# One pass fewer in the conversion of 64-bit weights, the state's step as one instruction, and a new table for the order

## The chip, the cores and the metric

One Trainium2 chip, one core. The metric is device time in microseconds of one execution, the median of several runs. The core has five engines that run side by side, each through its own queue in order: TensorE (PE, matmuls), VectorE (DVE), ScalarE (ACT), GpSimd (POOL) and SyncE (SP), which here issues most DMAs. Semaphores tie the queues together.

## The reference

Three layers follow each other, and only the last one's result is returned.

```
state = 0                                         # per batch and head: 48 x 48
for t in range(768):                              # 4 batches, 8 heads
    y[t] = r[t] @ (state + (u * k[t]) x v[t])     # x: outer product
    state = w[:, None] * state + k[t] x v[t]
x = y as 3072 tokens of 384
h = x @ w_in                                      # 384 -> 1024
s = h * softmax(h);  ln = (s - mean(s)) / sqrt(var(s) + 1e-6) * g_ln
x = ln @ w_out                                    # 1024 -> 384
e = argmax(x @ w_gate);  p = softmax(x @ w_gate)[e]        # 8 experts
out = p * (relu(x @ w1[e]) @ w2[e])
```

`w_in` and `w_out` reach the kernel as 64-bit floats; everything else is 32 bits wide.

## The kernel before

Tokens go in 24 tiles of 128 (six to a batch). **The first stage** turns a tile of `r`, `k`, `v` (`load_rkv`, issued by SyncE) into attention output: `kpow`, `ruk`, `asum`, `aval` make the factors, `rtrans` and `ktrans` transpose on TensorE, `rev` and `kev` copy the transposes out (`rT`, `kT`), `scores` multiplies, `causal` masks the result into `AT` (L400), `ahi` and `alo` split it into two 16-bit parts, `vhi` and `vlo` do the same with `v`, `attend` multiplies with the values and with the decayed state, and `yout` adds it all up (L427). `update` makes the tile's `k x v`, `advance` (L439) adds it to the state in two instructions, one for each half of the partitions, and `decay` multiplies the state by its weights into `sdec`. The update is a block of 128x384 of which only the diagonal blocks are wanted; `wdec` is zero outside of them.

**The second stage** takes a finished tile through `xtrans`, `xhi`, `xlo`, `mm1` (18 matmuls, L474), `hmax`, `hexp`, `hsolu`, `hvar`, `hseed`, `zscale`, `zlo`, `ztrans`, `mm2` (24 matmuls, L559), `choose` to `place`, and `send`, which scatters the rows by expert to HBM. `mm1` needs all of `w_in`, `mm2` all of `w_out`.

**The weights** come in seven chunks, three of `w_in` (128x1024) and four of `w_out` (128x768). `conv` plans a load and the steps of `to_f32` for each; `to_f32` builds 32-bit floats from the two halves of each 64-bit word (`lo`, `hi`, every second word of `raw`): an absolute value on ScalarE (L167), then on VectorE a product that zeroes words too small for 32 bits (L169), two steps that place exponent, mantissa and sign (L172, L174) and one that adds the low bits (L176). `raw` has two buffers, `tmp` one. Then `win_hi`, `win_lo` (L191) split `w_in`, and `wout_g` to `wout_lo` (last step L253) scale, fold and split `w_out`.

**The third stage** runs the eight experts (`emm1`, `rhi`, `rlo`, `emm2`, `eout`, `esend`), with weights loaded and split by `weights`.

**A guard** stands beside this: `marks`, `flags` (TensorE, L658) and `judge` (VectorE, L664 to L675) make one flag from sums of squares, from `wbad` and from the counts of tokens. At the end every engine loads the flag (`values_load`, L1181) and, when it is set, a general path recomputes everything with plain loops. It isn't set for these inputs.

**The order** is written by a planner, `plan`: each step has an engine, a cost in us, predecessors and a due time, and a list schedule takes the step that can start first, ties within `EPS` by due time. The table `X` holds the due times' offsets and a few knobs (`DB` biases steps that may run on VectorE or GpSimd, marked "either"). The kernel issues its instructions in that order, and every engine's queue keeps it.

Of the kernel before, what the change touches and what calls it, by code (L numbers as in the profile page):

```python
# [8 lines left out]
F32 = mybir.dt.float32  # L9
# [6 lines left out]
AF = mybir.ActivationFunctionType  # L16
ALU = mybir.AluOpType
# [17 lines left out]
SA, SV, SZ, SW = 2.0 ** 10, 2.0 ** 9, 2.0 ** 8, 2.0 ** 10  # L35
# [5 lines left out]
def body(ctx, tc, r, k, v, w, u, w_in, w_out, g_ln, w_gate, w1, w2, out):  # L41
# [18 lines left out]
    def sml(name, slot=None):  # L60
# [24 lines left out]

    X = dict(ET=-429.78, GG=-233.7, SO=-294.91, FL=-505.75, OL=1, ybuf=10, tmp=1, rkv=3, LAT=0.06, SELF=0.05,
             PRE=1.4, EPS=0.06, TA=144.7, TB=237.7, TM=276.51, NA=8, NB=9, M0=1038.64, W0=81.15, TW=251.26,
             W1=-298.48, TV=171.34, PF=134.77, PW=224.32, F0=466.45, EL=3, e=3, S0=12.3, P0=10.1, D0=2.5,
             L0=140.96, L1=105.03, U0=108.15, KG=5.83, PT=2, ZT=-610.22, F2=261, TE=288.64, GA=-152.99,
             GW=-226.57, GN=-97.54, DB=-0.71, KS=5.09, K0=202.89, K1=-109.3, xtrans=-983.06, kev=-515.9,  # L90
             ahi=-247.51, vlo=-135.95, ruk=1202.87, attend=-89.6, choose=-323.29, xhi=-244.14, vhi=27.84,
             own=138.51, hvar=-317, hmax=-289.95, gexp=-194.8, ktrans=655.01, rtrans=830.4, hexp=357.44,
             ztrans=-337.98, asum=-344.06, rev=-225.55, xlo=-713.89, decay=439.69, alo=897.3, rank=107.2,
             ld=344.13, xrow=-508.46, mm2=767.79, causal=-1488.31, hseed=638.5, send=114.58, hsolu=83.6,
             yout=-62.13, zlo=360.17, scores=-213.79, square=539.99, place=100.24, ysquare=-70.93,
             advance=-563.07, update=-90.68, zscale=-828, hroot=-416.04, mm1=19.74, aval=-17.98, kpow=98.58)

# [23 lines left out]
    guard = const.tile([P, 2, NT], F32, name="guard")  # L121
    wbad = const.tile([P, 4], F32, name="wbad")
    ph1 = ctx.enter_context(ExitStack())
# [33 lines left out]

    def to_f32(t, n, is64, dst):

        dst.append(t[:, 0:n])  # L160
        if is64:
            words = t[:, 0:2 * n].bitcast(I32).rearrange("p (f w) -> p f w", w=2)
            lo, hi = words[:, :, 0], words[:, :, 1]
            tmp = cv.tile([P, 2, 1024], F32, tag="tmp", name="tmp", bufs=X["tmp"])
            hm, a = tmp[:, 0, 0:n].bitcast(I32), tmp[:, 1, 0:n].bitcast(I32)
            dst[-1] = a.bitcast(F32)
            A.activation(hm.bitcast(F32), hi.bitcast(F32), AF.Abs)  # L167
            yield
            V.scalar_tensor_tensor(hm.bitcast(F32), hm.bitcast(F32), 1.125 * 2.0 ** -15, hi.bitcast(F32),  # L169
                                   op0=ALU.is_ge, op1=ALU.mult)  # L170
            yield
            V.tensor_scalar(a, hm, 3, 0x3FFFFFF8, op0=ALU.logical_shift_left, op1=ALU.bitwise_and)  # L172
            yield
            V.scalar_tensor_tensor(a, hm, -0x40000000, a, op0=ALU.bitwise_and, op1=ALU.bitwise_or)  # L174
            yield
            V.scalar_tensor_tensor(a, lo, 29, a, op0=ALU.logical_shift_right, op1=ALU.bitwise_or)  # L176

    raw = {}
# [3 lines left out]

    def win_bits(c):
        raw["f", c] = f = []
        return to_f32(raw.pop(("i", c)), FF, w_in.dtype != F32, f)

# [8 lines left out]

    def wout_bits(c):
        raw["g", c] = f = []
        return to_f32(raw.pop(("o", c)), 2 * DM, w_out.dtype != F32, f)

# [79 lines left out]
    def tables():

        t4 = [P, 4]
        for j in range(2):
            SP.dma_start(out=wc[64 * j:64 * j + D, :], in_=w.rearrange("(j two) d -> two d j", two=2)[j])
        V.tensor_copy(wbad, wc)
        V.tensor_scalar(wc, wc, WLO, WHI, op0=ALU.max, op1=ALU.min)
        V.tensor_tensor(wbad, wbad, wc, op=ALU.not_equal)
        tt = rot.tile([P, 4, P], F32, name="tt", tag="kT")
# [624 lines left out]
    for i in range(NT):  # L912
# [422 lines left out]
```

## Time and profile before

| | us |
|---|---|
| median of 3 runs | 634.06 |
| lowest and highest run | 633.23, 634.15 |
| profiled execution | 634.09 |
| its span, first to last instruction | 632.4 |
| TensorE busy | 578.8 |
| VectorE busy | 455.9 |
| ScalarE busy | 347.9 |
| GpSimd busy | 272.0 |

The profiled execution lies 1.7 us above its span and agrees with the median. Busy shares over the whole span average three stages with different limits, so the profile is to be read stage by stage; the row of an engine's own wait names who ended it.

### The profile page before, as it was taken

To read this page: it belongs to the slowest core of one execution; us is meant where nothing else is said; L and a number is where in the kernel's file an instruction comes from. 1 tells how busy PE (TensorE), PEld (TensorE's weight loads), DVE (VectorE), ACT (ScalarE), POOL (GpSimd) and SP (SyncE) were. 2 spreads that over 40 slices of the span, in tenths; PEclk is the share of its full clock that TensorE was granted. 3 is DMA by queue.
4 is the path that set the end of the run, shared out by engine and by line. 5 is a ranking of instruction groups with operands and counts; after the bars stand their busy time and mean duration, and the time that the engine had idled before them with its cause. 6 is when DMAs were issued, how large, how long until landed. Compare 5 with 4: busy or idle time off the path is not lost.

```text
span 632.4 us, 10941 instructions
## 1 busy us (share of the span) xinstructions
PE 578.8 (92%) x4037; PEld 497.1 (79%) x4037; DVE 455.9 (72%) x799; ACT 347.9 (55%) x577; POOL 272.0 (43%) x435
## 2 busy tenths in 40 slices
PE   2767887999999999999999989999999999999992
PEld 2667776867777777778877648998889999999992
DVE  7999989998798888888875655447665767578010
ACT  2754557379777676777756753445252535345210
POOL 3778767746755865665535452110001021001211
PEclk9876978999999999999999989999999999999997
DMA  9943736994565592947044624735455675764110
GB/s 170 227 109 60 157 93 198 238 160 93 99 116 95 106 129 54 154 72 129 28 76 98 196 100 163 273 107 189 129 182 161 200 203 170 208 141 108 52 38 23
DMA packets 163185, 83.79 MB, mean 132 GB/s; under 512 B 140100, under 2 KB 156346, under 8 KB 162736
## 3 DMA queue, kind: packets, MB, share of 16 engines
q1 hardware_dynamic: 159808, 73.51, 51.7%
q0 software_dynamic: 3312, 9.47, 4.5%
q8 instruction: 34, 0.56, 0.4%
q14 instruction: 31, 0.25, 0.1%
HBM read 51.71 MB, written 16.30 MB: 108 GB/s over the span
## 4 chain that ended last, share of the span: by engine, by line
PE 52%; DVE 17%; issue 10%; DMA 10%; POOL 4%; ACT 4%; POOLq 0%; SPq 0%; ACTq 0%; DVEq 0%
PE emm L772 12%; PE mm L559 10%; PE mm L474 9%; DMA out<-o,gt 8%; PE emm L815 7%; PE emm L797 3%; PE scores L396 2%; PE update L433 2%; DVE AT L400 2%; PE attend L419 2%; DVE tmp L169 2%; DVE tmp L174 2%; PE etrans L753 1%; DVE vl L369 1%; PE attend L422 1%
## 5 line engine op out<-in xcount | busy, mean ns | idle before, releaser
L847 POOL DMA_INDIRECT out<-o,gt x30 | 30.1, 1003 | 206.8 <-ACT o L843 104.3
L559 PE MATMUL mm<-wo,zT 128*128 128x392 f16 x576 | 100.7, 332 | 0.5 <-DVE zT L550 0.4
L474 PE MATMUL mm<-wi,xh 128*128 128x512 f32 x288 | 91.8, 400 | 3.3 <-DVE AT L400 3.3
L559 PEld LDWEIGHTS <-zT 128*128 128x128 f16 x576 | 55.9, 98 | 38.4 <-issue 1.3
L783 ACT ACTIVATE hh<-emm 128x896 fp32r<-128x896 f32 (+7 forms) x32 | 28.2, 882 | 82.3 <-PE emm L772 79.6
L786 DVE SCALAR_TENSOR_TENSOR hl<-emm,hh 128x896 fp32r<-128x896 f32 (+7 forms) x32 | 33.4, 1044 | 55.2 <-ACT hh L783 55.2
L772 PE MATMUL emm<-exh,w1h 128*128 128x256 f32 (+8 forms) x216 | 73.1, 338 | 0.0
L772 PE MATMUL emm<-exh,w1l 128*128 128x256 f32 (+8 forms) x216 | 72.6, 336 | 0.0
L772 PE MATMUL emm<-exl,w1h 128*128 128x256 f32 (+8 forms) x216 | 72.6, 336 | 0.0
L474 PEld LDWEIGHTS mm<-wi,xh 128*128 128x128 f32 x288 | 52.7, 189 | 13.6 <-DVE AT L400 3.7
L474 PE MATMUL mm<-wi,xl 128*128 128x512 f32 x144 | 56.5, 392 | 0.0
L815 PE MATMUL emm<-hh,w2h 128*128 128x480 f32 (+4 forms) x120 | 43.8, 365 | 0.0
L815 PE MATMUL emm<-hh,w2l 128*128 128x480 f32 (+4 forms) x120 | 43.1, 359 | 0.0
L815 PE MATMUL emm<-hl,w2h 128*128 128x480 f32 (+4 forms) x120 | 43.1, 359 | 0.0
L613 POOL DMA_INDIRECT xs<-row,pos x24 | 29.7, 1236 | 30.0 <-issue 13.8
L396 PE MATMUL scores<-rT,kT 64*128 64x128 f32 x384 | 32.5, 317 | 11.0 <-DVE st L494 7.7
L772 PEld LDWEIGHTS emm<-exh,w1l 128*128 128x128 f32 x216 | 40.7, 189 | 1.4
L772 PEld LDWEIGHTS emm<-exh,w1h 128*128 128x128 f32 x216 | 40.8, 189 | 1.4
L772 PEld LDWEIGHTS emm<-exl,w1h 128*128 128x128 f32 x216 | 40.8, 189 | 1.3
L396 PEld LDWEIGHTS scores<-rT,kT 64*128 64x128 f32 x384 | 27.4, 216 | 15.4 <-issue 7.0
L500 ACT ACTIVATE z<-e,st 128x1024 f16<-128x1024 f32 x24 | 27.5, 1145 | 18.0 <-DVE st L494 11.0
L480 DVE TENSOR_REDUCE st<-mm 128x1 f32<-128x1024 f32 x24 | 29.3, 1220 | 10.6 <-PE mm L474 9.2
(208 smaller groups left out, 1566.0 us busy)
## 6 DMA issues: line engine op xcount, KB each, us to landing
stage<-in_moe_w SPq DMA_DIRECT2D x16, 768.0 KB, 4.8
stage<-in_moe_w SPq DMA_DIRECT2D x8, 1024.0 KB, 5.0
xs<-zf SPq DMA_DIRECT2D x8, 772.0 KB, 12.2
rkv<-in_r SPq DMA_DIRECT2D x24, 192.0 KB, 4.9
rkv<-in_k SPq DMA_DIRECT2D x24, 192.0 KB, 5.1
rkv<-in_v SPq DMA_DIRECT2D x24, 192.0 KB, 4.5
stage<-in_moe_w SPq DMA_DIRECT2D x8, 512.0 KB, 4.2
xg<-xs SPq DMA_DIRECT2D x5, 772.0 KB, 6.4
```

Of the source, the lines that this page charges most:

```text
L396: T.matmul(ps[:, a, j * P:(j + 1) * P], kT[h, j, :], rT[h, j, :], start=True, stop=True)
L474: T.matmul(ps[:, n, :], a[:, j, :], wi[b][:, j, n * 512:(n + 1) * 512], start=(j == 0 and m == 0), stop=(j == KD - 1 and m == 2))
L480: V.tensor_reduce(st[:, 0:1], tk["h", i], op=ALU.max, axis=AX.X, negate=True)
L500: A.activation(z[:, 0, :], tk["e", i], AF.Square, scale=-float(FF), bias=st[:, 2:3], accum_out=st[:, 4:5])
L559: T.matmul(ps[:, 0:OW], zz[:, a, c, :], wo[b][:, c, :], start=(c == 0 and m == 0), stop=(c == KF - 1 and m == 2))
L613: G.indirect_dma_start(out=xs, out_offset=bass.IndirectOffsetOnAxis(ap=pos.bitcast(U32), axis=0), in_=row, in_offset=None, bounds_check=E ...
L772: T.matmul(ps[:, x, :], a[:, j, fc * P:(fc + 1) * P], b[:, j, :], start=(j == 0 and m == 0), stop=(j == KD - 1 and m == 2))
L783: A.activation(cols(d, "hh", q), d["pm", q], AF.Relu)
L786: V.scalar_tensor_tensor(cols(d, "hl", q), d.pop(("pm", q)), 0.0, cols(d, "hh", q).bitcast(F32), op0=ALU.max, op1=ALU.subtract)
L797: T.matmul(ps[0:n, 0:DM], a[:, c, j * P:j * P + n], b[:, c, :], start=(c == 0 and m == 0), stop=(c == KF - 1 and m == 2))
L815: T.matmul(ps[:, 0:d["nr"]], a[:, c, m * P:(m + 1) * P], b[:, c, :], start=(c == 0 and x == 0), stop=(c == KF - 1 and x == 2))
L847: G.indirect_dma_start(out=out, out_offset=bass.IndirectOffsetOnAxis(ap=d["gt"][0:n, j, 1:2].bitcast(U32), axis=0), in_=d.pop(("o", j))[0: ...
```

## The change

`to_f32` drops the product L169. Two of the remaining three VectorE passes read `hi` in `raw` itself instead of the product in `tmp`. ScalarE, after the absolute value, computes Relu(threshold - |hi|) and sums it along the row into a new column of `wbad`, which grows from 4 to 12 columns; a sum above zero sets the guard's flag. On the general path (`small is None`) the four passes stay. `advance` becomes one instruction over all 128 partitions and 384 columns. The costs that the planner is told follow, `marks` waits for the conversions, and all of the table `X` is new.

```diff
-    wbad = const.tile([P, 4], F32, name="wbad")
+    wbad = const.tile([P, 12], F32, name="wbad")
+    thr = const.tile([P, 1], F32, name="thr")
...
+    G.memset(wbad, 0.0)
+    G.memset(thr, 1.125 * 2.0 ** -15)
...
-            V.scalar_tensor_tensor(hm.bitcast(F32), hm.bitcast(F32), 1.125 * 2.0 ** -15, hi.bitcast(F32),
-                                   op0=ALU.is_ge, op1=ALU.mult)
+            if small is None:
+                V.scalar_tensor_tensor(hm.bitcast(F32), hm.bitcast(F32), 1.125 * 2.0 ** -15, hi.bitcast(F32),
+                                       op0=ALU.is_ge, op1=ALU.mult)
+                hi = hm
+            else:
+                A.activation(hm.bitcast(F32), hm.bitcast(F32), AF.Relu, scale=-1.0, bias=thr, accum_out=small)
             yield
-            V.tensor_scalar(a, hm, 3, 0x3FFFFFF8, op0=ALU.logical_shift_left, op1=ALU.bitwise_and)
+            V.tensor_scalar(a, hi, 3, 0x3FFFFFF8, op0=ALU.logical_shift_left, op1=ALU.bitwise_and)
             yield
-            V.scalar_tensor_tensor(a, hm, -0x40000000, a, op0=ALU.bitwise_and, op1=ALU.bitwise_or)
+            V.scalar_tensor_tensor(a, hi, -0x40000000, a, op0=ALU.bitwise_and, op1=ALU.bitwise_or)
             yield
             V.scalar_tensor_tensor(a, lo, 29, a, op0=ALU.logical_shift_right, op1=ALU.bitwise_or)
...
     def advance(i):
-        p4 = tk.pop(("pu", i))[:, 0:DM].rearrange("p (j a d) -> p j a d", j=4, a=2)
-        for a in range(2):
-            h = slice(64 * a, 64 * a + 64)
-            if i % NC == 0:
-                V.tensor_scalar(state[h, :, a, :], p4[h, :, a, :], SV, None, op0=ALU.mult)
-            else:
-                V.scalar_tensor_tensor(state[h, :, a, :], p4[h, :, a, :], SV, sdec[h, :, a, :], op0=ALU.mult, op1=ALU.add)
+
+        flat, ps = state.rearrange("p j a d -> p (j a d)"), tk.pop(("pu", i))[:, 0:DM]
+        if i % NC == 0:
+            V.tensor_scalar(flat, ps, SV, None, op0=ALU.mult)
+        else:
+            V.scalar_tensor_tensor(flat, ps, SV, sdec.rearrange("p j a d -> p (j a d)"), op0=ALU.mult, op1=ALU.add)
...
-        op(("bits", kind, c), "", [("act", 1.15 * t), ("dve", 1.4 * t), ("dve", 1.3 * t), ("dve", 1.4 * t), ("dve", 1.4 * t)] if F64 else [("dve", .01)],
+        op(("bits", kind, c), "", [("act", 1.15 * t), ("act", 1.15 * t), ("dve", 1.1 * t), ("dve", 1.4 * t), ("dve", 1.4 * t)] if F64 else [("dve", .01)],
...
-            op(("advance", i), "dve", .71, [("update", i), ("decay", i - 1), ("decay", i - 2)], advance, i, first=f + X["advance"])
+            op(("advance", i), "dve", .55, [("update", i), ("decay", i - 1), ("decay", i - 2)], advance, i, first=f + X["advance"])
...
-    X = dict(ET=-429.78, GG=-233.7, SO=-294.91, FL=-505.75, OL=1, ybuf=10, tmp=1, rkv=3, LAT=0.06, SELF=0.05,
+    X = dict(ET=-29.23, GG=-120.46, SO=-383.87, FL=374.6, OL=1, ybuf=10, tmp=1, rkv=3, LAT=0.06, SELF=0.05,
...
```

Where instructions stand now, at three places.

VectorE at the beginning, from the last of the tables (`trT`, L313) into the first tiles, before:

```order
L313 TENSOR_SCALAR trT<-trT 128x512
L627 MEMSET koff 128x1
L169 SCALAR_TENSOR_TENSOR tmp<-tmp,raw 128x1024
L172 TENSOR_SCALAR tmp<-tmp 128x1024
L347 TENSOR_TENSOR kp_116<-rkv_118,tkm 128x8x48
L369 SCALAR_TENSOR_TENSOR vl<-rkv_118,vh 128x384
L383 TENSOR_TENSOR rT<-rtrans,trT 128x512
L174 SCALAR_TENSOR_TENSOR tmp<-tmp 128x1024
L442 TENSOR_SCALAR state<-update 64x4x48 x2
```

and after, where `trT` (L322) is thirteen instructions ahead of the first L181 and the rows begin with the first tile's `au`:

```order
L366 TENSOR_REDUCE au<-ru 128x8
L378 SCALAR_TENSOR_TENSOR vl<-rkv_122,vh 128x384
L409 TENSOR_TENSOR AT<-scores,mask 128x1024
L392 TENSOR_TENSOR rT<-rtrans,trT 128x512
L366 TENSOR_REDUCE au<-ru 128x8
L418 TENSOR_TENSOR al<-AT,ah 128x1024
L409 TENSOR_TENSOR AT<-scores,mask 128x1024
L181 TENSOR_SCALAR tmp<-raw 128x1024
L392 TENSOR_TENSOR rT<-rtrans,trT 128x512
L183 SCALAR_TENSOR_TENSOR tmp<-raw,tmp 128x1024
L452 SCALAR_TENSOR_TENSOR state<-update,sdec 128x384
L185 SCALAR_TENSOR_TENSOR tmp<-raw,tmp 128x1024
```

The first pass over a chunk stood directly behind the tables (a memset apart) and stands behind the first attention steps of two tiles now; the three passes follow each other within five rows.

VectorE at the end of the program, where `hl` is a step of the last expert and `fli` the guard's flag, before:

```order
L786 SCALAR_TENSOR_TENSOR hl<-emm_6679,hh 128x2x368
L786 SCALAR_TENSOR_TENSOR hl<-emm_6703,hh 128x2x368
L786 SCALAR_TENSOR_TENSOR hl<-emm_6726,hh 128x2x368
L786 SCALAR_TENSOR_TENSOR hl<-emm_6750,hh 128x2x368
L1181 TENSOR_LOAD fli
```

and after, where the last `hl` and the first of `judge` (L672) stand just ahead:

```order
L673 TENSOR_SCALAR guard<-flags 128x24
L674 TENSOR_REDUCE fl<-guard 128x1
L675 TENSOR_SCALAR fl<-fl 128x1
L676 TENSOR_TENSOR guard<-keys,kcap 128x8
L677 TENSOR_SCALAR guard<-flags 128x1
L678 TENSOR_REDUCE fl<-guard 128x1
L679 TENSOR_SCALAR fl<-flags 128x1
L680 TENSOR_TENSOR fl<-fl,flags 128x1
L681 TENSOR_TENSOR fl<-fl 128x1
L682 TENSOR_TENSOR fl<-fl 128x1
L683 CAST fli<-fl 128x1
L1189 TENSOR_LOAD fli
```

The instructions of `judge` stood within the first expert before and are VectorE's last now, ahead of its load of the flag.

TensorE at the end of the program, where `emm` is the last expert's second product, before:

```order
L797 MATMUL emm_6831<-w2h,hl 112x384
L797 MATMUL emm_6831<-w2h,hh 112x384
L797 MATMUL emm_6831<-w2l,hh 112x384
L797 MATMUL emm_6831<-w2h,hl 112x384
L1181 TENSOR_LOAD fli
```

and after:

```order
L805 MATMUL emm_6798<-w2l,hh 112x384
L805 MATMUL emm_6798<-w2h,hl 112x384
L666 MATMUL flags<-guard,mask 128x48
L667 LDWEIGHTS ones_71
L667 MATMUL flags<-cum,ones_71 128x8
L668 LDWEIGHTS ones_71
L668 MATMUL flags<-cuma,ones_71 128x1
L1189 TENSOR_LOAD fli
```

The matmuls of `flags` moved from the first expert's first product to behind the last expert's last matmul.

## Rows read from the trace of the kernel before

**Rows 1.** The page's part 2: busy tenths of VectorE in 40 equal slices.

```profile
DVE  7999989998798888888875655447665767578010
```

**Rows 2.** Busy time by stage (stretch, length, engines, granted clock, DMA share, GB/s).

```profile
9.20:134.50 125.30, 100.14 (x842) 89.09 (x843) 120.14 (x163) 70.61 (x121) 87.68 (x73) 0.88 0.75 159
...
134.50:378.00 243.50, 237.14 (x1836) 179.27 (x1837) 193.87 (x410) 177.98 (x315) 146.11 (x306) 0.99 0.56 104
...
378.00:620.60 242.60, 241.50 (x1361) 228.73 (x1358) 136.16 (x188) 96.60 (x140) 34.53 (x41) 1.00 0.51 152
```

**Rows 3.** VectorE's groups, 0 to 134.5 us (busy us, mean ns | idle before).

```profile
L400 DVE TENSOR_TENSOR AT<-scores,mask 128x1024 f32<-128x1024 f32 x10 | 12.2, 1218 | 0.4 <-PE scores L396 0.3
...
L369 DVE SCALAR_TENSOR_TENSOR vl<-rkv,vh 128x384 f16<-128x384 f32 x11 | 12.1, 1096 | 0.3 <-ACT vh L365 0.3
...
L169 DVE SCALAR_TENSOR_TENSOR tmp<-tmp,raw 128x768 f32<-128x768 f32 (+1 forms) x7 | 11.1, 1581 | 0.1
...
L383 DVE TENSOR_TENSOR rT<-rtrans,trT 128x512 f32<-128x512 f32 x10 | 6.8, 680 | 0.4 <-PE rtrans L374 0.4
...
L357 DVE TENSOR_REDUCE au<-ru 128x8 f32<-128x384 f32 x11 | 6.0, 543 | 0.1
...
L444 DVE SCALAR_TENSOR_TENSOR state<-update,sdec 64x192 f32<-64x192 f32 x16 | 5.6, 350 | 0.9 <-PE update L433 0.8
...
L427 DVE SCALAR_TENSOR_TENSOR av<-attend,av 128x384 f32<-128x384 f32 x10 | 5.5, 550 | 1.0 <-PE attend L422 0.8
...
L361 DVE TENSOR_TENSOR av<-rkv,au 128x384 f32<-128x384 f32 x6 | 5.1, 862 | 0.0
```

**Rows 4.** Lines of the conversion (ns: least, median, most; first, last start).

```profile
L169 DVE SCALAR_TENSOR_TENSOR tmp<-tmp,raw x7: 949/1256/3149, 9.8 to 107.1; 128x768 f32<-128x768 f32 x4, 128x1024 f32<-128x1024 f32 x3
...
L172 DVE TENSOR_SCALAR tmp<-tmp x7: 545/1022/2321, 11.0 to 108.4; 128x768 int32<-128x768 int32 x4, 128x1024 int32<-128x1024 int32 x3
...
L176 DVE SCALAR_TENSOR_TENSOR tmp<-raw,tmp x7: 943/1208/1732, 20.7 to 113.3; 128x768 int32<-128x768 int32 x4, 128x1024 int32<-128x1024 int32 x3
```

**Rows 5.** Timeline of VectorE and TensorE (start, length); last, a piece of the chain.

```profile
9.77 1.22 DVE L169 SCALAR_TENSOR_TENSOR tmp<-tmp,raw 128x1024 f32<-128x1024 f32 x1
...
10.95 1.09 PE L374 MATMUL rtrans<-ident,rkv 128*128 128x128 f32 x4 [0.62 <-ACT tkm L312]
...
134.52 8.12 PE L559 MATMUL mm<-wo,zT 128*128 128x392 f16 x48
...
166.30 0.36 PE L419 MATMUL attend<-sdec,rT 128*128 128x96 f32 x2
...
168.00 0.52 PE L457 MATMUL xtrans<-ident,av 128*128 128x128 f32 x3
...
172.78 0.60 PE L379 MATMUL ktrans<-ident,kp 128*128 128x128 f32 x4
...
173.13 0.71 PE L474 MATMUL mm<-wi,xh 128*128 128x512 f32 x2
...
177.41 1.16 PE L396 MATMUL scores<-rT,kT 64*128 64x128 f32 x16
...
194.26 0.86 PE update L433 x8
```

**Rows 6.** The flag and the end (timeline; last two: ns, then start us).

```profile
385.73 0.32 PE L658 MATMUL flags<-guard,mask 128*128 128x48 f32 x2
...
387.97 0.15 DVE L675 CAST fli<-fl 128x1 int32<-128x1 f32 x1
...
620.27 0.34 PE L797 MATMUL emm<-w2h,hl 128*112 128x384 f32 x1
...
622.17 0.95 POOL L847 DMA_INDIRECT out<-o,gt  x1 [2.75 <-DMA out<-o,gt]
...
L1181 POOLq TENSOR_LOAD <-fli x1: 504/504/504, 622.0 to 622.0; - x1
...
L1183 POOLq EVENT_SEMAPHORE  x6: 17/30/43, 625.3 to 625.7; - x6
```

More of the change, by code (lines that the diff above doesn't have):

```diff
@@ L84, in body @@
     V.memset(mhalf, -0.5)
-    X = dict(ET=-429.78, GG=-233.7, SO=-294.91, FL=-505.75, OL=1, ybuf=10, tmp=1, rkv=3, LAT=0.06, SELF=0.05,
[L87 to L96, printed above, removed]
@@ new lines, in body @@
+    X = dict(ET=-29.23, GG=-120.46, SO=-383.87, FL=374.6, OL=1, ybuf=10, tmp=1, rkv=3, LAT=0.06, SELF=0.05,
+             PRE=1.4, EPS=0.1, TA=176.56, TB=248.64, TM=254.17, NA=8, NB=9, M0=495.42, W0=42.93, TW=105,
+             W1=-530.44, TV=257.99, PF=664.51, PW=-382.4, F0=-386.07, EL=3, e=3, S0=12.3, P0=10.1, D0=2.5,
+             L0=-679.5, L1=615.58, U0=13.12, KG=9.92, PT=2, ZT=-247.56, F2=148.59, TE=84.91, GA=118.81,
+             GW=-220.86, GN=157.31, DB=-1.5, KS=8.04, K0=610.2, K1=199.94, xtrans=-970.71, kev=571.15,
+             ahi=622.76, vlo=9.17, ruk=307.19, attend=625.35, choose=-170.33, xhi=-20.99, vhi=706.01,
+             own=263.22, hvar=668.67, hmax=132.27, gexp=-753.32, ktrans=-390.29, rtrans=539.68, hexp=150.63,
+             ztrans=70.39, asum=173.22, rev=-2168.6, xlo=-650.67, decay=77.28, alo=655.25, rank=-472.96,
+             ld=-228.91, xrow=-249.65, mm2=1203.62, causal=-107.84, hseed=-596.66, send=-284.2, hsolu=-201.28,
+             yout=597.49, zlo=288.89, scores=540.82, square=141.08, place=-51.35, ysquare=-575.28,
+             advance=-342.55, update=136.08, zscale=-399.78, hroot=-622.85, mm1=452.87, aval=631.76,
+             kpow=460.49)
@@ L156, in raw_load, with to_f32 @@
         return t
-    def to_f32(t, n, is64, dst):
+    def to_f32(t, n, is64, dst, small):
         dst.append(t[:, 0:n])
@@ L181, in win_load, with win_bits @@
         raw["i", c] = raw_load(w_in, c, 1)
-    def win_bits(c):
+    def win_bits(c, count=True):
         raw["f", c] = f = []
-        return to_f32(raw.pop(("i", c)), FF, w_in.dtype != F32, f)
+        return to_f32(raw.pop(("i", c)), FF, w_in.dtype != F32, f, wbad[:, 4 + c:5 + c] if count else None)
     def win_hi(c):
@@ L194, in wout_load, with wout_bits @@
         raw["o", c] = raw_load(w_out, c, 2)
-    def wout_bits(c):
+    def wout_bits(c, count=True):
         raw["g", c] = f = []
-        return to_f32(raw.pop(("o", c)), 2 * DM, w_out.dtype != F32, f)
+        return to_f32(raw.pop(("o", c)), 2 * DM, w_out.dtype != F32, f, wbad[:, 8 + c // 2:9 + c // 2] if count else None)
     def wout_g(c):
@@ L259, in fold_all @@
             win_load(c)
-            run(win_bits, c)
+            run(win_bits, c, False)
             win_hi(c)
@@ L264, in fold_all @@
             wout_load(c)
-            run(wout_bits, c)
+            run(wout_bits, c, False)
             wout_g(c)
@@ L283, in tables @@
             SP.dma_start(out=wc[64 * j:64 * j + D, :], in_=w.rearrange("(j two) d -> two d j", two=2)[j])
[L284 removed]
+        V.tensor_copy(wbad[:, 0:4], wc)
         V.tensor_scalar(wc, wc, WLO, WHI, op0=ALU.max, op1=ALU.min)
[L286 removed]
+        V.tensor_tensor(wbad[:, 0:4], wbad[:, 0:4], wc, op=ALU.not_equal)
         tt = rot.tile([P, 4, P], F32, name="tt", tag="kT")
@@ L970, in body @@
     b_left = set(ops)
-    last = [(n, i) for n in ("place", "ysquare", "square", "causal") for i in range(NT)]
+    last = [("bits", "i", c) for c in range(KD)] + [("bits", "o", c) for c in range(0, KF, 2)] + [(n, i) for n in ("place", "ysquare", "square", "causal") for i in range(NT)]
     op("count", "pe", .06, [("place", i) for i in range(NT)], count, bank="s", until=[("sort", 0)], first=X["SO"])
```

## The prediction

> **What bounds the kernel now.** I read the busy shares along the span first, then the same by stage. VectorE is at nine tenths or more in nearly all of the first eight slices of forty [rows 1]. Cut where TensorE starts its first `mm2` (134.52 us [rows 5]), the stages have different limits [rows 2]: from 9.2 to 134.5 us VectorE is busy 120.1 of 125.3 us while TensorE has 100.1, at a granted clock of 0.88; from 134.5 to 378 us TensorE is busy 237.1 of 243.5 us, VectorE 193.9; from 378 to 620.6 us TensorE has 241.5 of 242.6. So the end is the first `mm2` plus a nearly full TensorE, and a VectorE instruction is worth its length only before 134.5 us. The profiled execution took 634.09 us for a span of 632.4, the median of the runs is 634.06: a change of the span is a change of the time.
>
> **The removed pass.** The seven L169 instructions cost 11.1 us in that stage [rows 3]. They range from 949 to 3149 ns [rows 4]. Undisturbed they would be four of 0.95 and three of 1024 columns at 1.22 (the AT pass of that size [rows 3]), 7.5 us; the other 3.6 us are waits. Because a GpSimd instruction that held L169 up may hold up the next VectorE instruction instead, I give half back: 1.8 us, bounds 0 and 3.6.
>
> What the trace shows is a spread of one shape by more than three. The Trainium skill, "SBUF — State Buffer", section "SBUF: two separate sides", says that VectorE and GpSimd lock a port pair for a whole instruction, and that a VectorE instruction with two SBUF inputs is of the kind that must wait. The rows agree as far as they go: L444, with one input from PSUM, shows none of the spread in its mean of 350 ns. By that page two of the three passes that stay have two SBUF inputs as well; if all 3.6 us came back through them, the time would be 630.9 us.
>
> **The first remaining pass** now reads every second word (`hi` in `raw`) where L172 read a packed tile. At the plain rate a stride costs nothing visible: L176 reads `lo` that way and has 943 ns at the least. But L172's least is 545 ns, a faster form [rows 4]. Kept, the cost is 0; lost, four times 0.40 and three times about 0.2 (1.22 against the median of 1.02), 2.2 us. I take 0, because nothing else in the instruction changes, and keep 2.2 as the other end.
>
> **ScalarE** gets seven Relu with a sum, about as long as the seven Abs of L167 plus 0.19 for reading the accumulator: 8 us. It is busy 70.6 of 125.3 us in the stage [rows 2], and nothing but the next use of `tmp` waits for them: cost 0; without that cover it would be up to 8 us, one per chunk.
>
> **The state's step.** Two halves of 0.35 us become one of 128x384, for which yout (L427, one PSUM and one SBUF input, same size) has 0.55 [rows 3]: 0.15 us saved each. Twenty steps, of which only those before the first `mm2` count.
>
> **The order** is the larger part. Counted along VectorE's rows up to the last `wo` low part (L253, L262 after), the new order has done less attention by then. Before and after: AT 10 and 8, `vl` 11 and 8, `rT` 10 and 8, `au` 11 and 8, yout 9 and 5, `av` on VectorE 6 and 1, steps of the state 9 and 6, `al` on VectorE 0 and 2. By [rows 3]: L169 -11.1; the state 18 halves at 0.35 against 6 at 0.55, -3.0; `vl` -3.3; AT -2.4; `rT` -1.4; `au` -1.6; yout -2.2; `av` -4.3; `al` +2.4 (two at the 1.22 of an AT pass). Six other kinds change by one or two short instructions, three up and three down, and are left out as cancelling. Sum -26.9 us.
>
> Against that stands the start. Before, VectorE fills its wait for the first tile with conversion. After, the conversion begins thirteen instructions behind the tables, and the first of these needs the first transposed tile, whose transposes run from 10.95 to 12.04 us [rows 5], while L169 starts at 9.77 [rows 5]: 2.2 us idle, and I add 0.8 where the first AT waits for scores. So +3.0, bounds 0 and 4.
>
> First `mm2`: 134.5 - 26.9 + 1.8 + 3.0 = 112.4 us. TensorE then owes what was put off. Its own order at the first `mm2`, before and after: `mm1` 6 and 5, scores 10 and 8, update 10 and 7, `rtrans` and `ktrans` 11 and 8 each, `xtrans` 8 and 5, attend 10 and 8. Start to next start in a gapless stretch [rows 5]: `mm1` 4.28, attend 1.70, four transposes 0.35; scores 1.16, `xtrans` 0.52, update 0.86 as listed. 4.28 + 2 x 1.16 + 3 x 0.86 + 6 x 0.35 + 3 x 0.52 + 2 x 1.70 = 16.2 us. The state of 134.5 us is reached at 112.4 + 16.2 = 128.6: **5.9 us gained**. Nothing of it is the mere shift of work.
>
> The steps of the second stage stay on a TensorE with 6.4 us idle [rows 2], so the saving there is 0; the expert stage has 1.1 us idle, so its other interleaving is 0.
>
> **The end.** `flags` and `judge` leave 385.7 us for the place behind the last matmul of TensorE. Before, every engine loaded the flag when it ran out of work, GpSimd last: load at 622.0 us for 0.50, and its next event behind the branch at 625.3 [rows 6]. Now no engine can branch before `judge` is done. From the first flags matmul (385.73) to the end of the last judge row (387.97 + 0.15) are 2.39 us; the last expert matmul starts at 620.27, so flags at about 620.44, judge done 622.83, load over at 623.33 against 622.46: **+0.9 us**. Bounds: 0, if the last send (issued at 622.17) sets the end, and 2.4, if all of judge comes on top.
>
> What the trace shows is 2.8 us from GpSimd's branch at 622.5 to its next event. The Trainium skill, "Runtime: NRT & Kernel Launch", section "Instruction fetch mechanics", says that a taken branch out of the prefetched window must fetch its target first. This speaks against the change: all five engines would fetch at once. The row agrees with a fetch, no row shows five together; with the 2.4 of the bound the time would be 630.6 us.
>
> **Sum.** 634.09 - 5.9 + 0.9 = **629.1 us**. With the poor ends (1.8 more wait, 2.2 for the stride, 1.0 at the start, tail 2.4) it is 634.09 - 0.9 + 2.4 = 635.6; with the good ones (1.8, 3.0, tail 0) 634.09 - 10.7 = 623.4.
>
> **Rivals.**
> A, forecast: 625.5 to 632.8 us, chance 0.46.
> B, the good ends together: 623.4, below 625.5, chance 0.17. For it: 25 us of TensorE idle and the clock of 0.88 before the first `mm2` [rows 2]; a denser feed would also give clock back. Against: VectorE's new start.
> C, the pass is gone but its time isn't: GpSimd's holds move on, the stride loses the fast form, the tail eats the rest (0.9 gained, 0.9 lost): 634.1, within 0.2%, chance 0.17. That is also the case in which the three passes cost what four did.
> D, slower: TensorE starves in the second stage because attention runs less far ahead. Counted in its order, before the seventh `mm1` 10 tiles are attended before and 8 after; before the tenth 12 and 11; before the thirteenth 15 and 13. A late tile costs its `mm1` yout 0.55, transposes 0.52 and a ScalarE copy and a VectorE subtraction of the same 384 columns, about 0.55 each (estimate from yout): 2.2 us at most. Half of the 18 that follow paying 1.3 gives 11.7 us: 634.1 - 5.0 + 11.7 = 640.8. It decides from 6.3 us of new waits, 0.35 for each. For it: VectorE also inherits the put-off attention there and is 80% busy now; against: the idle of only 6.4 us shows that such waits are rare. Chance 0.20.
>
> **How the numbers follow.** Likeliest is A at 629.1. 0.2% is 1.3 us, about what a measurement of this kernel can tell from no change. Faster: A and B, 0.63; same: C, 0.17; slower: D, 0.20. The range 622.5 to 638.5 leaves out some 0.06 of B and 0.11 of D.
>
> **What would show it.** Right: the first `mm2` at 110 to 116 us; no fourth pass and VectorE still over 90% busy before; ScalarE up 8 us and no row waiting for its Relu; the second stage's TensorE idle at 5 to 9 us; judge as the last VectorE rows and 10 to 11 us after them. Wrong: a first `mm2` after 120 us (the start or the waits are larger), the first pass of 768 columns at 0.95 instead of 0.55, TensorE idle over 12 us in the second stage (D), or over 14 us from the last expert matmul to the end.

## The result, and the profile after

| | us |
|---|---|
| before, median of 6 runs (lowest, highest) | 634.11 (633.23, 634.94) |
| after, median of 6 runs (lowest, highest) | 628.51 (628.42, 631.10) |
| ratio, 95% interval | 0.9916, 0.9904 to 0.9928 |
| profiled execution of after, its span | 629.15, 627.4 |

The change makes the kernel 5.6 us faster; 629.1 was forecast. Executions of one kernel spread by 2 to 7 us here, the long ones mostly with a lower granted clock (last section), so each median below is given with its lowest and highest. Here are the busy times by stage after the change, cut at the first `mm2`, at the second stage's last row copy (`xrow`) and at the last expert copy (`o`). The columns are those of [rows 2].

```profile
9.20:116.30 107.10, 80.62 (x671) 70.00 (x671) 98.07 (x131) 68.93 (x112) 70.76 (x63) 0.87 0.70 170
116.30:373.60 257.30, 254.55 (x2023) 195.28 (x2024) 210.79 (x433) 189.42 (x337) 146.73 (x312) 1.00 0.51 107
373.60:613.20 239.60, 238.51 (x1345) 226.96 (x1343) 132.94 (x173) 96.54 (x141) 35.05 (x36) 1.00 0.52 153
```

The kernel before has the first of these cuts in [rows 2]; the other two there:

```profile
134.50:380.50 246.00, 239.64 (x1852) 180.84 (x1853) 195.01 (x413) 177.98 (x315) 148.45 (x311) 0.99 0.55 104
380.50:620.70 240.20, 239.02 (x1346) 227.17 (x1343) 135.02 (x186) 96.60 (x141) 32.20 (x37) 1.00 0.51 153
```

Stage by stage: 18.2 us less to the first `mm2`, 11.3 more from there to the last `xrow`, 0.6 less among the experts. From the last `o` to the end of the span it was 632.4 - 620.7 = 11.7 us and is 627.4 - 613.2 = 14.2, so 2.5 more. Sum: -18.2 + 11.3 - 0.6 + 2.5 = -5.0, the difference of the two spans.

VectorE's groups of the first stage after the change (busy us, mean ns | idle before), to be read against [rows 3, 4]:

```profile
L409 DVE TENSOR_TENSOR AT<-scores,mask 128x1024 f32<-128x1024 f32 x8 | 9.7, 1216 | 0.2
...
L378 DVE SCALAR_TENSOR_TENSOR vl<-rkv,vh 128x384 f16<-128x384 f32 x8 | 6.6, 830 | 4.5 <-ACT vh L374 4.5
...
L185 DVE SCALAR_TENSOR_TENSOR tmp<-raw,tmp 128x1024 int32<-128x1024 int32 x3 | 6.5, 2162 | 0.0
...
L200 DVE TENSOR_TENSOR wi<-tmp,wi 128x1024 fp32r<-128x1024 f32 x3 | 6.3, 2109 | 0.5 <-ACT wi L197 0.5
...
L183 DVE SCALAR_TENSOR_TENSOR tmp<-raw,tmp 128x1024 int32<-128x1024 int32 x3 | 4.5, 1513 | 0.0
...
L181 DVE TENSOR_SCALAR tmp<-raw 128x768 int32<-128x768 int32 x4 | 2.8, 706 | 0.0
...
L452 DVE SCALAR_TENSOR_TENSOR state<-update,sdec 128x384 f32<-128x384 f32 x5 | 2.7, 543 | 0.0
```

L181, L183 and L185 are the three passes, L452 is the state's step. `vl` has an idle of 4.5 us in front of it that no row of before has. Where it stands is seen in VectorE's timeline at the start (start, length, idle before):

```profile
6.02 0.10 DVE L302 TENSOR_TENSOR tt<-tt 128x4 f32<-128x4 f32 x1
10.57 0.56 DVE L378 SCALAR_TENSOR_TENSOR vl<-rkv,vh 128x384 f16<-128x384 f32 x1 [4.45 <-ACT vh L374]
11.05 0.16 DVE L302 TENSOR_TENSOR tt<-tt 128x4 f32<-128x4 f32 x1
...
14.24 0.42 DVE L322 TENSOR_SCALAR trT<-trT 128x512 f32<-128x512 f32 x1
17.30 0.69 DVE L392 TENSOR_TENSOR rT<-rtrans,trT 128x512 f32<-128x512 f32 x1 [2.64 <-PE rtrans L383]
```

and in ScalarE's:

```profile
7.58 1.28 ACT L353 ACT_TABLE_LOAD   x1 [7.58 <-DMA rkv<-in_v]
8.87 1.16 ACT L353 ACTIVATE sq<-rkv 128x1152 bf16<-128x1152 f32 x1
...
10.04 0.51 ACT L374 ACTIVATE vh<-rkv 128x384 f16<-128x384 f32 x1
```

The first tile's `vl` stands in the middle of the tables (VectorE's powers of the decay, `tt` to `trT`). It waits for `vh`, which stands behind a load of ScalarE's own function table (1.28 us) and a square on ScalarE, and these wait for the load of `v`. The tables are done at 14.7 us instead of 9.85, and the first `rT` starts at 17.3 instead of 14.06.

The end, by each queue's branch behind the flag (line; count: ns; start) and the event that follows it:

```profile
L1191 SPq EVENT_SEMAPHORE  x9: 17/17/17, 620.2 to 620.8; - x9
L1191 POOLq EVENT_SEMAPHORE  x6: 17/30/43, 620.3 to 620.8; - x6
...
L1191 ACTq EVENT_SEMAPHORE  x2: 17/17/17, 619.7 to 619.8; - x2
L1191 DVEq EVENT_SEMAPHORE  x2: 21/21/21, 621.3 to 621.4; - x2
L1191 ACTq COMPARE_BRANCH  x1: 50/50/50, 616.1 to 616.1; - x1
L1191 POOLq COMPARE_BRANCH  x1: 53/53/53, 616.1 to 616.1; - x1
L1191 SPq COMPARE_BRANCH  x1: 53/53/53, 616.2 to 616.2; - x1
L1191 PEldq COMPARE_BRANCH  x1: 3369/3369/3369, 616.3 to 616.3; - x1
L1191 DVEq COMPARE_BRANCH  x1: 72/72/72, 616.5 to 616.5; - x1
```

All branch within 0.4 us of each other. GpSimd's next event comes 4.2 us behind its branch, where it was 2.8 [rows 6]. In between, the core's DMA engines carry instructions: six packets start between 617.05 and 617.56 us, within 1.5 us of the branches, and the longest lasts 2.1 us, up to 619.6. The earliest of the next events stands at 619.7. The view of 617 to 618 us (packets, MB, share of the engines):

```profile
q14 instruction: 5, 0.04, 24.6%
q8 instruction: 1, 0.02, 6.4%
```

### The profile page after: what moved, and what is told of

Read it like the earlier page. It is cut to its first block, busy times and chain, and to the rows that moved or that the text cites. A ratio compares the mean times of both kernels' runs of the same rounds, so it can differ in the third digit from the quotient of the medians.

```text
span 627.4 us, 10956 instructions
## 1 busy us (share of the span) xinstructions
PE 573.8 (91%) x4037; PEld 492.2 (78%) x4037; DVE 448.2 (71%) x781; ACT 357.1 (57%) x591; POOL 256.3 (41%) x428
## 5 line engine op out<-in xcount | busy, mean ns | idle before, releaser
L855 POOL DMA_INDIRECT out<-o,gt x30 | 33.0, 1100 | 202.4 <-ACT o L851 98.4
L482 PE MATMUL mm<-wi,xh 128*128 128x512 f32 x288 | 93.8, 408 | 0.6 <-DVE AT L409 0.6
L482 PEld LDWEIGHTS mm<-wi,xh 128*128 128x128 f32 x288 | 54.1, 194 | 11.4 <-DVE AT L409 0.8
L621 POOL DMA_INDIRECT xs<-row,pos x24 | 28.3, 1179 | 24.7 <-issue 13.8
L528 ACT ACTIVATE e<-e,st 128x1024 f32<-128x1024 f32 x22 | 27.3, 1241 | 19.4 <-POOL st L524 19.4
L428 PE MATMUL attend<-sdec,rT 128*128 128x96 f32 x160 | 36.7, 316 | 0.1
L717 DVE TENSOR_TENSOR w2l<-stage,w2h 128x768 fp32r<-128x768 f32 x32 | 30.1, 950 | 8.2 <-ACT w2h L715 8.2
L715 ACT ACTIVATE w2h<-stage 128x768 fp32r<-128x768 f32 x32 | 26.1, 842 | 14.0 <-PE emm L823 13.2
```

The source lines that it names most:

```text
L428: T.matmul(ps[:, j * 96:j * 96 + 96], rT[:, j, :], sdec[:, j].rearrange("p a d -> p (a d)"), start=True, stop=False, skip_group_check=True)
L482: T.matmul(ps[:, n, :], a[:, j, :], wi[b][:, j, n * 512:(n + 1) * 512], start=(j == 0 and m == 0), stop=(j == KD - 1 and m == 2))
L528: A.activation(e, e, AF.Identity, scale=st[:, 10:11], bias=st[:, 11:12])
L621: G.indirect_dma_start(out=xs, out_offset=bass.IndirectOffsetOnAxis(ap=pos.bitcast(U32), axis=0), in_=row, in_offset=None, bounds_check=E ...
L717: V.tensor_tensor(lo, d[:, x], hi.bitcast(F32), op=ALU.subtract)
L855: G.indirect_dma_start(out=out, out_offset=bass.IndirectOffsetOnAxis(ap=d["gt"][0:n, j, 1:2].bitcast(U32), axis=0), in_=d.pop(("o", j))[0: ...
```

## The experiments

The mark used below is the start of the first `mm2`, besides the time; in the changed kernel it is 116.34 us. A ratio is to the kernel before, measured beside it, with its 95% interval.

**1. The code in the old order.** The table and the planner's costs of before (and its predecessors of `marks`) under the changed code; one pass is moved by hand.

```
-    X = dict(ET=-29.23, GG=-120.46, SO=-383.87, FL=374.6, OL=1, ybuf=10, tmp=1, rkv=3, LAT=0.06, SELF=0.05,
+    X = dict(ET=-429.78, GG=-233.7, SO=-294.91, FL=-505.75, OL=1, ybuf=10, tmp=1, rkv=3, LAT=0.06, SELF=0.05,
...
     order, done = plan()
+    row = next(r for r in order if r[2] == (("bits", "i", 0), 2))
+    order.remove(row)
+    order.insert([r[2] for r in order].index(("rev", 0)) + 1, row)
```

> The changed code (three passes, the Relu count, the state's step as one instruction) in the order of before: its table and the costs its planner was told; only the first pass of the first chunk stands three rows later, behind the first rT, because it would otherwise stand ahead of the tables. Theory 1, what VectorE saves before the first mm2 reaches the end where the order doesn't give it away: L169 -11.1, half of its waits back +1.8, nine state steps -1.35, about +1.5 at the start where L169 and L172 filled a wait: first mm2 at about 125.3 us, and as TensorE's order is the same it owes nothing: 634.1 - 9.2 = 625 us. Theory 2, TensorE or the loads hold the stage as soon as VectorE is shorter: half of it, first mm2 at 129 to 130, 629 to 630 us. Theory 3, the gain of the changed kernel is the order's: 632 to 634 us.

Measured: 629.99 us (627.59 to 632.02), ratio 0.9938 (0.9919 to 0.9957), first `mm2` at 129.1. Theory 2. The first stage:

```profile
9.20:129.10 119.90, 95.01 (x842) 83.55 (x842) 108.93 (x140) 77.56 (x134) 85.59 (x73) 0.91 0.80 166
```

VectorE's busy time fell by 11.2 us, but its idle time rose from 5.2 to 11.0, so that only 5.4 us arrived at the first `mm2`. What it waited for:

```profile
DVE kp L355 <- ACT tkm L320: 5.3, 1, 5.3
DVE st L487 <- PE mm L481: 3.7, 2, 2.5
```

**2. The same with the start mended,** because `tkm` had come to stand behind the first Relu. The first chunk's Relu and two passes, the first square, `vh` and `vl` go behind the first `kT`.

```
     order, done = plan()
+    row = next(r for r in order if r[2] == (("bits", "i", 0), 1))
+    order.remove(row)
+    order.insert([r[2] for r in order].index(("kev", 0)) + 1, row)
...
```

> As code_only (the changed code in the order of before), with its start mended: the first chunk's Relu and the first tile's square and vh stand behind the first kT on ScalarE, so that tkm doesn't wait for them, and the first two passes and vl follow there on VectorE. In code_only VectorE waited 5.3 us for tkm and its first rT started at 16.5 us instead of 14.1. Theory 1: the 2.4 us come back, first mm2 at about 126.7, 627.5 us median; the new order is then worth nothing as it stands, and 5 us with its own start and tail mended (both). Theory 2, the old order loses them later in the stage (VectorE waited 3.7 us for mm1 in code_only): first mm2 at 129, 630 us. Theory 3, the old order is as good once the code is there: 623 us, the same as both.

Measured: 629.30 us (628.41 to 631.15), ratio 0.9929 (0.9907 to 0.9950); the first `rT` starts 4.2 us earlier than in experiment 1 (12.22 against 16.47 us), the first `mm2` at 129.4. Theory 2: the old order loses the start again, later in the stage.

```profile
9.20:129.40 120.20, 99.11 (x842) 87.21 (x843) 107.46 (x140) 77.33 (x134) 84.12 (x73) 0.89 0.81 166
```

VectorE is idle for 12.7 us. What it waited for:

```profile
DVE st L487 <- PE mm L481: 3.6, 2, 2.5
DVE vl L377 <- ACT vh L373: 2.4, 2, 2.2
DVE kp L355 <- DMA rkv<-in_k: 2.3, 1, 2.3
```

TensorE has the same 842 matmuls in front of the first `mm2` as before and needs 99 us of these 120 for them at a granted clock of 0.89. So in the old order no one engine holds this stage. That TensorE's longer list is what eats the saving is likely, but no run tests it by itself.

**3. The new order with the old code,** four passes and halves of the state.

```
-                A.activation(hm.bitcast(F32), hm.bitcast(F32), AF.Relu, scale=-1.0, bias=thr, accum_out=small)
+            V.scalar_tensor_tensor(hm.bitcast(F32), hm.bitcast(F32), 1.125 * 2.0 ** -15, hi.bitcast(F32),
+                                   op0=ALU.is_ge, op1=ALU.mult)
+            hi = hm
...
```

> The order of the changed kernel with the code of before (four passes with the product L169, no Relu, the state's step in two halves). Theory 1: seven products (11 us) and seven second halves (1 us) come back before the first mm2, which moves from 116.3 to about 128.5 us, and the end by as much: 640 us, so that the order alone would be a loss of 6. Theory 2, the first stage has slack and half of it is hidden: 634 us. Theory 3, the order alone is the gain: 630 us or less.

Measured: 639.86 us (639.51 to 641.42), ratio 1.0092 (1.0075 to 1.0109), first `mm2` at 126.8. Theory 1: the order alone loses 5.7 us, and in this order the code is worth 11.3 us (639.86 - 628.51). By the ratios, each to the kernel before on its own chip, it is 11.2 us, or 9.9 with the second set of the changed kernel (0.9936, experiment 6). In the old order it was worth 4.2 (experiment 1) and 5.4 (experiment 2).

```profile
9.20:126.80 117.60, 85.08 (x672) 72.40 (x673) 107.69 (x145) 61.48 (x98) 70.14 (x63) 0.85 0.65 155
```

The product's seven rows in this order:

```profile
L174 DVE SCALAR_TENSOR_TENSOR tmp<-tmp,raw 128x768 f32<-128x768 f32 x4 | 4.5, 1130 | 0.0
...
L174 DVE SCALAR_TENSOR_TENSOR tmp<-tmp,raw 128x1024 f32<-128x1024 f32 x3 | 4.3, 1424 | 0.0
```

Only 672 matmuls stand ahead of the first `mm2`, 85.1 of 117.6 us, and what the code saves on VectorE (107.7 - 98.1 = 9.6 us busy) arrives: with the new code the first `mm2` starts 10.5 us earlier.

**4. The start of the changed kernel mended:** the first `vl` behind the first `rT`, the second square behind the first `kT`.

```
     order, done = plan()
+    row = next(r for r in order if r[2] == ("vlo", 0))
+    order.remove(row)
+    order.insert([r[2] for r in order].index(("rev", 0)) + 1, row)
+    row = next(r for r in order if r[2] == ("square", 1))
+    order.remove(row)
+    order.insert([r[2] for r in order].index(("kev", 0)) + 1, row)
```

> The changed kernel with two instructions moved: the first tile's vl (L378) from the middle of the tables to behind the first rT, and the second tile's square on ScalarE from ahead of tkm to behind the first kT. In the changed kernel VectorE waits 4.45 us for vh with the tables half done, and 2.64 us for rtrans later. Theory 1: the tables end about 4.4 us earlier, the first rT starts at about 13 us instead of 17.3, everything on VectorE follows, first mm2 at about 112 us, end at 624.5 us. Theory 2, the loads or TensorE take the place of that wait within the stage: first mm2 at 115 to 116, 627.5 to 628.5 us.

Measured: 628.32 us (624.36 to 629.84), ratio 0.9901 (0.9874 to 0.9927). The profiled execution is a short one, 625.09 us; in it the first `rT` starts at 12.52 us and the first `mm2` at 112.31.

```profile
9.45 0.42 DVE L322 TENSOR_SCALAR trT<-trT 128x512 f32<-128x512 f32 x1
12.52 0.69 DVE L392 TENSOR_TENSOR rT<-rtrans,trT 128x512 f32<-128x512 f32 x1 [2.65 <-PE rtrans L383]
```

In the profiled execution the marks are those of Theory 1 (about 13 and about 112), but only two of six runs had the gain; the other four lie at 628 to 630. That median speaks for Theory 2.

**5. The flag judged early again.**

```
-FL=374.6
+FL=-505.75
```

> The changed kernel with the due time of marks, flags and judge as before (they run behind the second stage and not behind the last matmul); two pairs of ScalarE instructions swap with it. Theory 1: from the start of the last expert matmul to the end 11.8 us as before instead of 13.2, and each engine's branch is followed by its next event after 2.7 to 3.4 us instead of 3.4 to 4.8: 627.2 us, a gain of 1.3. Theory 2, the engines that branch together cost nothing and only the chain of judge counts: a gain of 0.9 as predicted, 627.6 us, with branches still 3.4 to 4.8 us long. Theory 3, the last send sets the end anyway or the flags' matmuls make TensorE wait in the middle for as much: 628.5 us.

Measured: 627.68 us (626.59 to 628.44), ratio 0.9891 (0.9870 to 0.9912). The last `o` starts at 614.76 us of a span of 626.7: 11.9 us to the end instead of 14.2. GpSimd:

```profile
L1191 POOLq EVENT_SEMAPHORE  x6: 17/30/43, 619.6 to 620.0; - x6
...
L1191 POOLq COMPARE_BRANCH  x1: 53/53/53, 616.9 to 616.9; - x1
```

Last `o` to GpSimd's branch: 2.1 us against 2.9; branch to next event: 2.7 against 4.2; from there to the end 7.1 in both. Theory 1 in the profile: 0.8 us are judge's chain, 1.5 us come with five engines branching at once. The span is only 0.7 us shorter all the same, because in this execution the first `mm2` came at 117.64, 1.3 us later. Over all profiles but that of experiment 7, six with judge early and five with judge last, the stretch from the last `o` is 11.6 to 12.6 and 14.1 to 14.5 us, and GpSimd's from its branch to the next event 2.7 to 2.9 and 3.9 to 4.4. The gain in the median, 0.8 us, is less than the runs resolve.

**6. Without the count.** The seven Relu are left out.

```
-                A.activation(hm.bitcast(F32), hm.bitcast(F32), AF.Relu, scale=-1.0, bias=thr, accum_out=small)
```

> The changed kernel without the seven Relu on ScalarE: words too small for 32 bits are not counted, the guard's columns for them stay zero. Theory 1, the count is hidden as forecast: 628.5 us within 0.2%, first mm2 within 1 us of 116.3, VectorE's rows unchanged. Theory 2, the Relu delays what ScalarE does next (ah, vh, wi's high part) and through these VectorE: up to one Relu, 1.15 us, for each of the four to seven chunks: 622 to 625 us. Theory 3: with the Relu away the first pass comes earlier but the order waits elsewhere: no change either, with the idle in other rows.

Measured: 632.67 us (628.56 to 635.49), ratio 0.9969 (0.9942 to 0.9996). Beside it **the changed kernel again:**

> The changed kernel once more, on the chip of the runs beside it: 628.5 us, so that each of the others can be read against it; from the last eout to the end 14.2 us, GpSimd's next event 4.2 us behind its branch.

631.20 us (628.48 to 633.53), ratio 0.9936 (0.9911 to 0.9961). Both medians lie above the 628.5 that was expected: of the twelve runs without the count, six with a granted clock of 0.956 or 0.957 took 633.6 to 635.5 us and six with 0.967 to 0.970 took 628.6 to 631.8. So the profile, of a run of 629.31 us, has to decide. Leaving out ScalarE's 7.6 us gains nothing:

```profile
9.20:116.20 107.00, 81.85 (x671) 70.67 (x671) 98.48 (x131) 61.38 (x98) 71.85 (x63) 0.86 0.74 168
```

ScalarE has 61.4 instead of 68.9 us, the first `mm2` comes at 116.24 instead of 116.34: hidden, Theory 1.

**7. What lengthens VectorE's rows.** Every step with a choice goes to VectorE.

```
-DB=-1.5
+DB=-1000
```

> The changed kernel with every step that may run on either engine planned on VectorE (the bias DB made so large that GpSimd is never chosen); the order follows from that. Asked here: what lengthens VectorE's rows. Theory 1, a VectorE row with two inputs from SBUF, or of the fast form, waits for the GpSimd instruction in flight: what rows of the conversions, vl, sdec, wi and wo have above the shortest of their shape, 11.6 us before the first mm2 in the changed kernel and 20.9 in the kernel before, falls under 2 us. Theory 2, it comes from DMA writes into SBUF or from the semaphores' own time: it stays at 8 us or more. The time is slower either way, since VectorE gets some 50 instructions of 0.55 to 1.2 us more before the first mm2: about 645 to 655 us.

Measured: 699.29 us, one run. What VectorE's rows from 9.2 us to the first `mm2` have above the shortest of their line and shape there, summed: 21.0 us before, 13.1 after, 14.5 in experiment 3, 1.1 here (the expectation has 20.9 and 11.6 for the first two); in the conversion, `vl`, `sdec`, `wi` and `wo` alone 17.9, 11.9, 13.4 and 0.3. GpSimd is busy for 14 us of this stretch here, against 70.8 after. The DMA share is 0.78 here and 0.70 after, so DMA writes aren't the cause: Theory 1. The time expected was some 45 us too low: the order came out otherwise, and the planner put 232 filler matmuls (L1063 `keep`) on TensorE, 50.2 us from 413.8 us on, which no other run has. The same groups as above, here:

```profile
L200 DVE TENSOR_TENSOR wi<-tmp,wi 128x1024 fp32r<-128x1024 f32 x3 | 3.7, 1222 | 0.0
L185 DVE SCALAR_TENSOR_TENSOR tmp<-raw,tmp 128x1024 int32<-128x1024 int32 x3 | 3.7, 1221 | 0.1
L378 DVE SCALAR_TENSOR_TENSOR vl<-rkv,vh 128x384 f16<-128x384 f32 x5 | 2.9, 577 | 4.4 <-ACT vh L374 4.4
L181 DVE TENSOR_SCALAR tmp<-raw 128x768 int32<-128x768 int32 x4 | 2.2, 551 | 0.0
L181 DVE TENSOR_SCALAR tmp<-raw 128x1024 int32<-128x1024 int32 x3 | 2.1, 684 | 0.0
```

L200 falls from 2109 to 1222 ns, L185 from 2162 to 1221, `vl` from 830 to 577. One such wait in the changed kernel, VectorE and then GpSimd:

```profile
32.49 2.76 DVE L200 TENSOR_TENSOR wi<-tmp,wi 128x1024 fp32r<-128x1024 f32 x1
35.17 2.48 DVE L378 SCALAR_TENSOR_TENSOR vl<-rkv,vh 128x384 f16<-128x384 f32 x1
37.58 0.54 DVE L366 TENSOR_REDUCE au<-ru 128x8 f32<-128x384 f32 x1
```

```profile
32.04 5.20 POOL L418 TENSOR_TENSOR al<-AT,ah 128x1024 f16<-128x1024 f32 x2
```

Two `al`, 5.2 us together, hold first `wi`, then `vl`: the first `al` ends at 34.17 us and `wi` 1.1 us later, the second at 37.24 and `vl` 0.4 us later. The Trainium skill, "SBUF — State Buffer", section "SBUF: two separate sides", names such a lock between the two engines for rows with two SBUF inputs and for the fast two-port form. These rows agree for two inputs, and L181, one input and a least of 541 ns, took up to 1491 ns in the changed kernel and at most 686 here, which agrees for the fast form.

**8. Both repairs in one:** `vl` and the squares of the first two tiles out of the way of `vh` and `tkm`, and the flag early.

```
-FL=374.6
+FL=-505.75
...
+    row = next(r for r in order if r[2] == ("square", 0))
+    order.remove(row)
+    order.insert([r[2] for r in order].index(("kev", 0)) + 1, row)
...
```

> The changed kernel with the first tile's vl behind the first rT as in start, but the squares of the first two tiles behind their kT on ScalarE, so that neither vh nor tkm waits for them, and with marks, flags and judge behind the second stage as in flag_fl. Theory 1, the two places are independent: 4.0 us from the first rT on (it starts at 12.5 to 13) and 2.0 us of the tail (11.9 us from the last eout to the end instead of 14.2): first mm2 at about 112.3, 622.5 us. Theory 2, the spread of start (624.4 to 629.8) comes from its start, where tkm still waited for a square that waits for a load; with the squares moved the runs lie together at 622 to 623.5. Theory 3, the spread comes from elsewhere in the first stage: median about 626, with runs from 622 to 628.

Measured: 622.88 us (621.54 to 624.67), ratio 0.9814 (0.9788 to 0.9839), first `mm2` at 111.49, 11.6 us behind the last `o`: Theory 1, and Theory 2 as it seemed. Then once more, on another chip:

> both once more, beside code_clean on the same chip: 622.9 us median, 621.5 to 624.7, first mm2 at 111.5, from the last eout to the end 11.6 us.

626.37 us (622.60 to 628.73), ratio 0.9857 (0.9827 to 0.9887). The spread is back, so Theory 2 of the first set falls: the squares weren't its cause, and it comes from elsewhere (Theory 3). Both intervals lie below those of the changed kernel (0.9904 to 0.9928 and 0.9911 to 0.9961): this version beats both kernels.

## Why the prediction was right, point by point

**What bounds the stages** held. VectorE is busy 98.1 of 107.1 us before the first `mm2`, TensorE 254.6 of 257.3 behind it.

**The removed pass** held in its size: -11.1 + 1.8 = -9.3 us were forecast. Experiment 3 against the change has 107.69 - 98.07 = 9.6 us of VectorE, of which seven state steps make 1.1 (14 halves at 0.35 against seven at 0.54): 8.5. Experiment 1 against before has 11.2, less 1.5 for ten steps and 1.0 for five short rows that stand outside its window: 8.7. That waits come back through other rows was right, and their cause is shown (experiment 7). That it is half of them isn't: in the old order such waits sum to 21.0 us with the product and 20.3 without it, so most of its 3.6 came back; in the new one the product takes only 8.8 us (experiment 3), and all but 0.3 of that is saved. What the prediction didn't see is that the new order itself takes a third off such waits, 21.0 to 14.5 us with the old code still in it. The largest shares are the conversion's own rows, 11.4 to 6.4, and `vl`, 6.1 to 2.8 with eight instead of eleven.

**The stride** costs nothing: the least of L181 is 541 ns for 768 columns, as L172 had 545 [rows 4], and undisturbed its means are 551 and 684 (experiment 7).

**ScalarE and the state's step** held: cost 0 (experiment 6), and 0.543 us for a whole step against 0.55 taken. The step alone, 1.1 us, was read from rows and not timed by itself.

**The order's sum** of -26.9 + 1.8 = -25.1 us held exactly: VectorE's busy time fell by 22.1 us in the window, and 3.0 us of tables had moved into it, which in before lay ahead of 9.2 us. That it is exact is luck: with fewer waits the conversion's rows fell by 12.9 instead of 9.3 us and `vl` by 5.4 instead of 3.3, while other kinds, which the sum left out, rose by 4.4 in all (`wi` +2.3, `sdec` +2.1, `z` +1.7, `wo` +1.5, `kp` -2.0, `st` -1.2).

**The start is the step that failed:** "So +3.0, bounds 0 and 4". It was 6.9: those 3.0 us of tables and 3.9 us more of idle (107.1 - 98.1 = 9.0 against 5.2). The prediction looked at the instructions between the last table and the first pass, not at `vl`, which the new order put inside the tables. So the first `mm2` came at 116.3 and not at 112.4; with `vl` moved it came at 112.31 (experiment 4) and 111.49 (experiment 8), or at 116.62 in the long execution of experiment 8 (last section).

**What TensorE owes** held: 16.2 us were forecast, its busy time from the first `mm2` to the last `xrow` rose by 14.9 (254.55 - 239.64). A part of the missing 1.3 may be that before's TensorE ran at a granted clock of 0.80 and 0.77 from 372 to 380 us, after's at 1.00 from 365 to 373.6.

**"The saving there is 0"** failed in the other direction: TensorE's idle time behind the first `mm2` fell from 6.4 to 2.75 us. It is the order's doing: experiment 3, with the old code, has 2.75 as well (258.9 - 256.15), experiment 1, with the old order, 4.6. So rival D, in which attention running less far ahead starves TensorE, had it the wrong way round, and the prediction's own sign, 5 to 9 us of idle, was missed.

**The end** was under-sized: 0.9 forecast, 2.5 measured, just past the bound of 2.4. The chain through judge has about its 0.9 (2.9 against 1.8 us from the last `o` to GpSimd's branch); the other 1.4 are the branch itself, 4.2 against 2.8 us. From the last expert matmul (612.76 us) to the end of the span it is 14.6 us, past the 14 that the prediction had named as a sign of being wrong. The sentence set beside the sum had the direction. The Trainium skill, "Runtime: NRT & Kernel Launch", section "Instruction fetch mechanics", says that a taken branch whose target isn't prefetched waits for a transfer of it. The trace agrees: instruction packets follow the branches, and in the changed kernel five engines wait at once, for 3.4 to 4.8 us. In experiment 5 GpSimd's branch at 616.9 us has only two such packets behind it before its next event, 0.5 and 0.4 us long. That the transfers slow each other is likely, but not shown by itself.

So the total was right to 0.6 us by luck, because four errors cancel: +3.9 at the start, +1.6 at the end, against about -4.9 of TensorE behind the first `mm2` (3.6 of idle, 1.3 of busy time) and -0.6 among the experts. The closeness is the set's too: the second set of the same kernel has a median of 631.20 us (experiment 6).

## What to carry to other kernels

Price code and order together: the same saving on VectorE was worth 4 to 5 us in an order with 842 matmuls ahead of the first `mm2`, and 10 to 11 in one that had put 170 of them off. When a new order is adopted, read the first twenty instructions of every engine for one that waits for a load ahead of work that doesn't. A check that every engine reads at the end belongs early, where the engines come to it one after the other: the end was 11.6 to 12.6 us long that way and 14.1 to 14.5 the other.

## What the runs showed of the hardware

**The granted clock differs between executions of one program,** and the times with it, by as much as the change. The two executions of experiment 8 that were profiled, first the short, then the long:

```profile
9.20:111.50 102.30, 80.61 (x672) 70.08 (x673) 95.02 (x120) 68.50 (x111) 70.71 (x63) 0.87 0.79 178
```

```profile
9.20:116.60 107.40, 87.42 (x671) 74.86 (x672) 96.57 (x120) 68.48 (x111) 70.00 (x63) 0.81 0.71 170
```

The first `rT` starts at 12.43 us in both, VectorE's busy time is the same within 1.6 us, but TensorE needs 6.8 us more for the same matmuls at a granted clock of 0.81 instead of 0.87, and the first `mm2` comes 5.1 us later. From 30 to 40 us, behind a stretch in which TensorE was busy for a half to six tenths, both have 0.50 and 0.53, about the lower of its two levels, 1.2 GHz. They part behind that: from 40 to 50 us the granted clock is 0.89 in the short one and 0.62 in the long one, from 80 to 90 us 0.84 and 0.66. The changed kernel shows such a difference elsewhere, short and long execution:

```profile
117.00:120.00 3.00, 3.00 (x20) 1.77 (x19) 3.00 (x7) 1.12 (x3) 0.00 (x0) 1.00 0.01 3
```

```profile
117.00:120.00 3.00, 2.54 (x9) 1.21 (x10) 3.00 (x6) 0.58 (x2) 0.00 (x0) 0.60 0.96 107
```

In both, TensorE had waited 1.4 us in front of its first `mm2`; in one the clock stayed, in the other it fell. Why it falls in some executions and not in others stays open, and with it why four of six runs of experiment 4 didn't show the gain that the profile explains.

**Most engines that branch at once wait longer for their next event.** ScalarE has 2.6 to 2.8 us where the engines come one after the other and 3.6 to 4.3 where all come together, VectorE 2.9 to 3.7 and 4.3 to 5.0, GpSimd as in experiment 5. SyncE, 3.0 to 3.7 and 3.1 to 4.4, shows it in four profiles of five; TensorE, 3.4 to 4.4, shows no difference.
